# Two layers of attention and MLP on one core: the first row blocks of layer 1 pass over the keys in two spans instead of three

## The chip, the cores and the metric

One core of a Trainium2 chip runs the whole kernel. The metric is the device time of one execution in microseconds. Each time is a median of several runs; the profile is of one further execution, whose own time stands beside its span.

The engines are named as the profile names them: PE is TensorE, ACT is ScalarE, DVE is VectorE, POOL is GpSimd, SP is SyncE, whose queue (SPq) issues the DMAs here.

## The reference

The input x has 2048 rows of 448 columns. Two layers with the same weights are applied to it. Each adds an attention with 16 heads of 28 columns, and then an MLP with 1792 hidden columns.

```python
x = A_x
x = x + _A_ref(_layernorm(x, axis=-1), A_wqkv, A_wo)
x = x + _B_ref(_layernorm(x, axis=-1), B_w1, B_b1, B_w2, B_b2)
x = x + _A_ref(_layernorm(x, axis=-1), A_wqkv, A_wo)
x = x + _B_ref(_layernorm(x, axis=-1), B_w1, B_b1, B_w2, B_b2)
# _A_ref: qkv = x @ wqkv, p = softmax(q k^T * 28 ** -0.5), (p v) @ wo
# _B_ref: h = relu(x @ w1 + b1), (h * h) @ w2 + b2
```

Every one of the 2048 rows of a layer attends to all 2048 keys of that layer. A key of layer 1 exists only when layer 0 has finished that row, attention and MLP.

## The kernel before

**Tiling.** Rows are taken in row blocks of 256 (`blocks`, L242; the last two of layer 1 have 128), keys in 16 key blocks of 128. The 16 heads are four groups `g` of four heads `hh`, which lie on 32 partitions each. A *unit* is the scores of one head for a row block against two key blocks: 512 columns. Three units make one score tile `sc` of 1,536 columns in PSUM, of which there are two buffers. One exponential of ACT (L834) turns such a tile into `pt` in SBUF. There are 2,048 units in the two layers, and 683 tiles.

**Some units go to DVE.** `apart` (L703) can take one unit of a tile away from ACT: DVE then computes the exponential itself with a polynomial, in six instructions (L892, L904, three times L909, L915), and ACT gets a tile of 1,024 columns. `apart` allows it when DVE has been idle enough lately (`pl.load(SPAN, "DVE")`), with a lower bound when the MLP work is behind its line (`behind`, L688, with `LINES`).

**Passes.** `add_passes` (L652) lists the passes: a pass is one row block, one head group and one range of key blocks. A pass runs the units of its range, and then multiplies their exponentials with V into one PSUM tile `oT` (PV, L982). If the range is not the last one of the row block, `ev` (L996) moves `oT` to SBUF, into a part of `K_sb` of the other layer (`part`, L289): the first range copies (L1005), the later ones add (L1007). The last range adds the parts to `oT_sb`. Row blocks 0, 1 and 2 of layer 1 (`AHEAD`, L52) run over the keys in ranges given by `CUTS` (L93, L662): all three row blocks and four head groups over the first range, then all over the second, and so on. In this way layer 1 can begin while layer 0's MLP still makes the later keys. The other row blocks run over all 16 key blocks at once.

**After the last range** of two head groups, `norm_pair` (L1068) divides by the softmax's sum: a small DMA spreads the sums over partitions (`dn<-oT_sb`, L1080), DVE takes the reciprocal (L1085), a DMA writes it to DRAM (`scr<-dn`, L1091), another brings it back on all partitions (`rec<-scr`, L1099), and DVE multiplies (L1104). When the four groups are done, `chain` (L1116) does the rest of the layer for the row block: output projection, addition to x (L1113), layer norm (statistics L448, `rstd` on POOL L471, L520, transposes L493, copy L505), hidden layer (w1 on PE at L553, relu L1160, square L1167), w2, addition to x. In layer 0 it goes on to K, V and Q of layer 1 (L575, L603, L571).

**What sets the order.** `Planner` (L124) goes through all streams of work while the program is built. It keeps a clock for each engine, gives every operation a start from its inputs and its buffers, and emits them in that order; the instruction streams of all engines are fixed then, and each engine runs its own in order. The score stream has the first priority, ACT's exponentials the second, the PV stream (`p_stream`, L932) the third; MLP and projections fill in. A score tile needs its keys and queries (`needs`, L739) and a free `sc` buffer. Where PE has been idle lately, the score matmuls of a tile are issued again (`again`, L797), or matmuls with the identity are put in (`heat`, L1203, L1218): they change no result and keep PE busy.

Of the kernel before, what the change touches and what calls it, by code (L numbers as in the profile page):

```python
# [89 lines left out]
HSTOP = 0  # L90
CHUNK = 2
EV = 3.5
CUTS = (0, 8, 12, 16)  # L93


class Res:
# [121 lines left out]
def kernel(  # L218
# [433 lines left out]
    def add_passes(l, qbs, cuts, gs=range(G)):  # L652
        for lo, hi in zip(cuts, cuts[1:]):
            for qb in qbs:
                for g in gs:
                    passes.append((l, qb, g, range(lo, hi), lo == 0, hi == NTB))
# [3 lines left out]
    for qb in range(2, len(blocks[0])):  # L660
        add_passes(0, [qb], [0, 16])
    for cut in zip(CUTS, CUTS[1:]):  # L662
        for qb, gs in enumerate(AHEAD):
            add_passes(1, [qb], cut, gs)
        if cut[1] == CUTS[-2]:
            bridged = len(passes)
# [602 lines left out]
```

The softmax here doesn't subtract the row's maximum and nothing guards it: scores larger than these inputs give would overflow.

## Time and profile before

| | |
|---|---|
| median of 4 runs | 896.29 us (894.43 to 897.07) |
| profiled execution, its own time | 895.43 us |
| its span | 893.6 us |
| DVE busy | 794.0 us in 1,572 instructions |
| PE busy | 830.6 us in 12,829 matmuls |
| POOL busy | 39.0 us |
| all DMA | 18.43 MB, 21 GB/s on average |
| L834, full tiles | 555, of 1,536 columns |
| L834, short tiles | 128, of 1,024 columns |
| first exponential begins, last one ends | 9.4 and 877.6 us |

The exponentials are numbered 0 to 682 below in the order in which ACT runs them; the score tiles have the same numbers. Number 341 is the first with units of layer 1. In the profile, a row of the groups gives line, engine, operation, what is written and read with its shape, how often; then busy time, mean duration of one, and the idle time of that engine before it with what ended it. A duration of one exponential includes a part that overlaps the next one, so the distance of two starts is shorter than it.

### The profile page before, as it was taken

To read this page: it belongs to the slowest core of one execution; us is meant where nothing else is said; L and a number is where in the kernel's file an instruction comes from. 1 tells how busy PE (TensorE), PEld (TensorE's weight loads), DVE (VectorE), ACT (ScalarE), POOL (GpSimd) and SP (SyncE) were. 2 spreads that over 40 slices of the span, in tenths; PEclk is the share of its full clock that TensorE was granted. 3 is DMA by queue.
4 is the path that set the end of the run, shared out by engine and by line. 5 is a ranking of instruction groups with operands and counts; after the bars stand their busy time and mean duration, and the time that the engine had idled before them with its cause. 6 is when DMAs were issued, how large, how long until landed. Compare 5 with 4: busy or idle time off the path is not lost.

```text
span 893.6 us, 29098 instructions
## 1 busy us (share of the span) xinstructions
PE 830.6 (93%) x12829; PEld 458.3 (51%) x12829; DVE 794.0 (89%) x1572; ACT 878.8 (98%) x707; POOL 39.0 (4%) x98
## 2 busy tenths in 40 slices
PE   8999999998999999999989998888999999999998
PEld 4555654554545545454554554444544544545566
DVE  7988999999889999999889999889898999989654
ACT  8999999999999999999999999999999999999995
POOL 3100000000000000100000000001000000000000
PEclk9999999999999999999999999999999999999999
DMA  9100100000000000000000000011000000000100
GB/s 266 35 3 3 27 19 11 14 14 15 14 3 14 15 14 14 14 11 6 2 2 2 2 2 2 3 39 38 11 18 19 20 25 19 20 8 19 32 14 18
DMA packets 33915, 18.43 MB, mean 21 GB/s; under 512 B 18874, under 2 KB 33339, under 8 KB 33788
## 3 DMA queue, kind: packets, MB, share of 16 engines
q1 hardware_dynamic: 33788, 16.58, 6.6%
q8 instruction: 100, 1.64, 0.8%
q14 instruction: 27, 0.22, 0.1%
HBM read 14.26 MB, written 2.07 MB: 18 GB/s over the span
## 4 chain that ended last, share of the span: by engine, by line
ACT 68%; issue 12%; PE 11%; DVE 7%; DMA 2%; SPq 1%; POOL 0%; DVEq 0%
ACT pt L834 68%; PE mt L553 4%; PE sc L809 3%; PE oT L982 2%; DVE v_h L909 1%; DVE K_sb L909 1%; DVE r L1160 1%; DMA rec<-scr 1%; PE sc L553 1%; DVE st L448 1%; DVE oTn L1104 0%; SPq L303 0%; DMA dn<-oT_sb 0%; DMA x_sb<-in_A_x_dram 0%; DVE oT_sb L1007 0%
## 5 line engine op out<-in xcount | busy, mean ns | idle before, releaser
L834 ACT ACTIVATE pt<-sc 128x1536 bf16<-128x1536 f32 (+1 forms) x683 | 863.9, 1569 | 2.4 <-PE sc L809 2.1
L809 PE MATMUL sc<-Q_sb,K_sb 32*128 32x256 bf16 (+1 forms) x5848 | 324.9, 265 | 53.6 <-ACT pt L834 48.0
L809 PEld LDWEIGHTS <-K_sb 32*128 32x128 bf16 x5848 | 157.6, 92 | 229.7 <-issue 201.1
L982 PE MATMUL oT<-pt,V_sb 128*32 128x256 bf16 (+1 forms) x4094 | 151.9, 268 | 0.6 <-DVE xnT L505 0.3
L553 PE MATMUL mt<-xnT,w 128*128 128x256 bf16 (+1 forms) x928 | 120.6, 269 | 0.9 <-DVE r L1160 0.5
L982 PEld LDWEIGHTS <-V_sb 128*32 128x32 bf16 x4352 | 91.7, 96 | 47.3 <-issue 44.3
L909 DVE SCALAR_TENSOR_TENSOR K_sb<-K_sb 128x512 f32<-128x512 uint16 x165 | 112.9, 685 | 0.9 <-PE mt L553 0.2
L909 DVE SCALAR_TENSOR_TENSOR v_h<-v_h,v_i 128x512 f32<-128x512 f32 x144 | 98.2, 682 | 0.6
L553 PEld LDWEIGHTS <-w 128*128 128x128 bf16 x952 | 78.6, 98 | 35.5 <-issue 27.2
L1160 DVE TENSOR_SCALAR r<-mt 128x512 bf16<-128x512 f32 x106 | 72.2, 681 | 14.8 <-PE mt L553 14.5
L553 PE MATMUL mt<-w,V_sb 128*128 128x448 bf16 (+2 forms) x288 | 67.6, 345 | 0.0
L892 DVE TENSOR_SCALAR v_i<-sc 128x512 int32<-128x512 f32 x72 | 49.3, 685 | 9.7 <-PE sc L809 9.3
L1113 DVE TENSOR_TENSOR x_sb<-x_sb,mt 128x448 bf16<-128x448 bf16 (+2 forms) x63 | 37.8, 605 | 13.4 <-PE mt L553 13.4
L909 DVE SCALAR_TENSOR_TENSOR v_h<-v_i 128x512 f32<-128x512 uint16 x72 | 49.1, 682 | 0.5
L470 POOL TENSOR_TENSOR ve<-mv,eps_t 128x2 f32<-128x2 f32 (+1 forms) x34 | 8.8, 260 | 840.8 <-DVE mv L449 840.8
L1218 PE MATMUL mt<-xn,ident 128*128 128x448 bf16 x130 | 43.5, 357 | 0.5 <-DVE x_sb L1113 0.3
L892 DVE TENSOR_SCALAR K_sb<-sc 128x512 int32<-128x512 f32 x55 | 37.6, 684 | 4.5 <-PE sc L809 4.3
L448 DVE BATCH_NORM_STATS2 st<-x_sb 128x6 f32<-128x448 bf16 x64 | 39.4, 615 | 1.4 <-DMA x_sb<-in_A_x_dram 1.2
L553 PEld LDWEIGHTS <-V_sb 128*128 128x128 bf16 x302 | 24.8, 98 | 25.5 <-issue 11.2
L915 DVE SCALAR_TENSOR_TENSOR V_sb<-v_h,v_e 128x512 bf16<-128x512 f32 x46 | 31.4, 682 | 0.3
L1167 DVE TENSOR_TENSOR V_sb<-r 128x512 bf16<-128x512 bf16 (+1 forms) x69 | 28.7, 417 | 2.1 <-ACT r L1158 1.5
L904 DVE TENSOR_SCALAR v_e<-v_i 128x512 int16<-128x512 int16 x72 | 30.1, 418 | 0.0
(106 smaller groups left out, 733.4 us busy)
## 6 DMA issues: line engine op xcount, KB each, us to landing
rec<-scr SPq DMA_DIRECT2D x56, 128.0 KB
x_sb<-in_A_x_dram SPq DMA_DIRECT2D x8, 224.0 KB
out_dram<-x_sb SPq DMA_DIRECT2D x15, 112.0 KB
w<-in_B_w_dram SPq DMA_DIRECT2D x1, 1568.0 KB
w<-in_B_w_dram SPq DMA_DIRECT2D x1, 1344.0 KB
dn<-oT_sb SPq DMA_DIRECT2D x56, 4.0 KB
V_sb<-in_A_wqkv_dram SPq DMA_DIRECT2D x4, 168.0 KB
scr<-dn SPq DMA_DIRECT2D x28, 8.0 KB
```

Of the source, the lines that this page charges most:

```text
L448: nc.vector.bn_stats(out=st[:, :], in_=x_sb[:, t0 + j, :])
L553: nc.tensor.matmul(box["t"][:, c0:c0 + n], lhsT=lhsT() if callable(lhsT) else lhsT, rhs=rhs, start=a, stop=b)
L809: nc.tensor.matmul(dst[k][:, i * nt * P:(i + 1) * nt * P], lhsT=K_sb[l][rows, g, (kb + i) * P:(kb + i + 1) * P], rhs=Q_sb[rows, g, t0 * P: ...
L834: t = nc.scalar.activation(out=pt[:, 0:n], in_=gbuf[gi]["sc"][:, 0:n], func=AF.Exp, scale=float(np.log(2.0)) * 2.0 ** -FRAC)
L892: t = nc.vector.tensor_scalar(out=box["i"], in0=two(src), scalar1=EXP_BIAS, scalar2=EXP_LOW, op0=ALU.add, op1=ALU.max)
L904: nc.vector.tensor_scalar(out=box["e"], in0=box["n"], scalar1=128.0, scalar2=128.0 * EXP_FIELD, op0=ALU.mult, op1=ALU.add)
L909: nc.vector.scalar_tensor_tensor(out=box["h"], in0=box["f"] if begin else box["h"], scalar=b, in1=box["f"], op0=ALU.add, op1=ALU.mult)
L915: nc.vector.scalar_tensor_tensor(out=box["two"](pd), in0=box["h"], scalar=b0, in1=box["e"].bitcast(DT.bfloat16), op0=ALU.add, op1=ALU.mult)
L982: nc.tensor.matmul(box["t"][DHP * hh:DHP * hh + DHP, 0:n], lhsT=V_sb[l][:, kb + i, 4 * g + hh, :], rhs=p[:, c0:c0 + n], start=begin and kb ...
L1113: nc.vector.tensor_tensor(out=x_sb[:, tb, lo:hi], in0=x_sb[:, tb, lo:hi], in1=t[:, 0:hi - lo], op=ALU.add)
L1160: nc.vector.tensor_scalar(out=r[:, 0:w], in0=t[:, 0:w], scalar1=0.0, scalar2=None, op0=ALU.max)
L1218: nc.tensor.matmul(t[:, 0:D], lhsT=ident[:, :], rhs=xns[0][:, 0:D], start=True, stop=True)
```

## The change

```diff
--- before.py
+++ after.py
@@ -90,7 +90,7 @@
 HSTOP = 0
 CHUNK = 2
 EV = 3.5
-CUTS = (0, 8, 12, 16)
+CUTS = (0, 10, 16)
```

Row blocks 0, 1 and 2 of layer 1 now run over key blocks 0 to 9 first, and then over 10 to 15. Before, they ran over 0 to 7, then 8 to 11, then 12 to 15. Each of the 12 pairs of row block and head group thus has two passes instead of three: one copy and one addition instead of one copy and two additions. The planner then orders everything after the first tiles of layer 1 anew.

## Prediction

> **What bounds the kernel now.** I read the page's busy table first, then the chain, then the exponentials by shape.
>
> ```profile
> PE 830.6 (93%) x12829; PEld 458.3 (51%) x12829; DVE 794.0 (89%) x1572; ACT 878.8 (98%) x707; POOL 39.0 (4%) x98
> ACT 68%; issue 12%; PE 11%; DVE 7%; DMA 2%; SPq 1%; POOL 0%; DVEq 0%
> ...
> L834 ACT ACTIVATE pt<-sc 128x1536 bf16<-128x1536 f32 x555 | 776.0, 1649 | 1.8 <-PE sc L809 1.5 <-ACT pt L834 0.2
> L834 ACT ACTIVATE pt<-sc 128x1024 bf16<-128x1024 f32 x128 | 147.9, 1225 | 0.6 <-PE sc L809 0.6
> ```
>
> ScalarE (ACT) is the bound: busy for 878.8 of 893.6 us, nearly all of it in the 683 exponentials of L834. PE at 93% is no second bound, because some of its work is filler (score matmuls of L809 issued again, identity matmuls of L1218). So only three things can move the time: how many units of 512 columns ACT exponentiates, how long ACT stands still between exponentials, and the stretch after the last one. One unit handed to VectorE shortens an exponential from 1,649 to 1,225 ns, so it is worth 0.42 us; the starts in the timeline say the same (1.33 us after a full tile, 0.905 us after a shorter one).
>
> Then I looked for ACT's lost time in the half that the change touches. I number the exponentials 0 to 682 in their order. Layer 1 begins at 341, so all before that stands as it was: the two builds' orders first differ at score group 344 (448 us). The busy time by stretches (columns: length, PE, PEld, DVE, ACT, POOL, granted clock, DMA share, GB/s):
>
> ```profile
> 580.00:590.00 10.00, 8.33 (x136) 3.86 (x136) 9.94 (x21) 10.00 (x9) 0.00 (x0) 1.00 0.12 30
> 590.00:600.00 10.00, 8.23 (x144) 4.70 (x145) 7.46 (x17) 9.74 (x9) 0.00 (x0) 1.00 0.18 51
> 600.00:610.00 10.00, 8.72 (x136) 4.26 (x124) 9.96 (x21) 9.48 (x8) 0.00 (x0) 1.00 0.14 35
> ...
> 630.00:640.00 10.00, 9.36 (x152) 5.08 (x150) 10.00 (x21) 9.68 (x8) 0.00 (x0) 1.00 0.02 4
> ```
>
> ACT falls short only around 600 and 636 us. By starts, exponentials 460 to 479 take 592.78 to 619.38, 26.60 us, where 17 full and 3 short ones at 1.33 and 0.905 make 25.33: **1.27 us lost**. Exponentials 480 to 499, of the same mix, take 26.27: 0.94 lost. The timeline of VectorE, PE and ACT tells why for the first:
>
> ```profile
> 589.99 0.42 DVE L1007 TENSOR_TENSOR oT_sb<-oT,K_sb 128x256 f32<-128x256 f32 x1
> 590.17 1.13 SPq L1080 DMA_DIRECT2D dn<-oT_sb  x2
> 594.36 0.25 DVE L1085 RECIPROCAL dn<-dn 128x16 f32<-128x16 f32 x1 [1.82 <-DMA dn<-oT_sb]
> 598.14 0.68 DVE L915 SCALAR_TENSOR_TENSOR pd<-K_sb,v_e 128x512 bf16<-128x512 f32 x1
> 598.88 0.27 PE L982 MATMUL oT<-pd,V_sb 128*32 128x256 bf16 x1 [0.80 <-DVE pd L915]
> 599.93 1.02 ACT L834 ACTIVATE pt<-sc 128x1024 bf16<-128x1024 f32 x1 [0.26 <-PE sc L809]
> ```
>
> VectorE reaches the reciprocal of a normalization before its DMA has landed and stands 1.82 us; the exponential that it was computing itself (L915) is late behind it, the PV matmul on PE waits 0.80 us for that, the scores queued behind the PV matmul are late, and ACT idles. It happens where VectorE has no slack: its instructions in the order of exponentials 450 to 469, at their start-to-start times (0.60 us for L909 and its like, 0.33 for L1007), are 24.3 us against 24.2 us of ACT.
>
> **What the change removes.** Row blocks 0, 1 and 2 of layer 1 make 24 passes instead of 36, so 12 of the L1007 additions into K_sb go. This row is that operation:
>
> ```profile
> L1007 DVE TENSOR_TENSOR K_sb<-oT,K_sb 128x256 f32<-128x256 f32 x28 | 11.7, 416 | 3.2 <-PE oT L982 3.1
> ```
>
> 12 x 0.33 = 4.0 us of VectorE, none of it on ACT's path by itself. The matmuls of scores (repeats aside) and of PV, the DMAs and GpSimd's instructions are as many as before. The planner fills the room: in the changed build's order, ACT has 553 full and 130 short exponentials (before 555 and 128), so VectorE takes 129 units instead of 127. ACT gains 2 x 0.42 = **-0.85 us**. VectorE pays 2 x (5 x 0.60 + 0.33) = 6.7 us, plus 0.6 us for one relu of the end that moves from ACT to it: +3.3 us net on an engine at 89%, spread over 440 us.
>
> PE issues 92 fewer repeated score matmuls and 15 more identity ones: filler, in gaps. Here a rule speaks against the change. The Trainium skill (TensorE: Matmul & The Clock Gate, Part 1 and "HAM oscillation") says that a PE idle for a window of about 3.4 us falls to half clock. By the rule, a stretch such as exponentials 440 to 459, with 12.0 us of real PE work in 24.6 us, depends on its filler; at half clock its 0.88 us of score and PV matmuls for an exponential would become 1.8 us against 1.33, about 1.1 us lost for each such window. The row says a granted clock of 1.00 in every stretch, and in that stretch the repeated scores are more than before (252 score matmuls). I take 0.
>
> **What it moves: the end of the first passes.** Each pass of the last span is 12 units (4 exponentials) instead of 8 (2.7). Two passes make one normalization, so these come every 8 exponentials (10 us) instead of 5.3 (6.7 us), each with its DMAs dn, scr and rec and its two VectorE steps. In the new order VectorE's densest 20 exponentials of layer 1 are 380 to 399 (24.3 us in 25.1), then 460 to 479 (23.9 in 25.5) and 410 to 429 (22.8 in 24.2): no 20 are full. The first row block's MLP also starts some 10 exponentials earlier, where PE and VectorE had room. So I take the 1.27 us as gone: **-1.27 us**. This rests on the DMA's real delay: from the end of L1007 (590.41) to the reciprocal (594.36) the row shows 3.95 us. The skill's fixed cost of about 2.0 us (DMA: Bandwidth & Descriptors, "Anatomy of one DMA", given for another issuing path) would have had it land before VectorE arrived at 592.5; by it there was no such wait to remove, and the gain would be 0. I take the row. Ends: 0 and -2.2 (the 0.94 goes as well; I leave it, since the same w1 and relu work comes in any case).
>
> **What it moves: keys 14 and 15 of layer 1.** The second span now holds keys 10 to 15, so keys 14 and 15 are needed at exponential 424 instead of 439, 15 x 1.26 = 19 us earlier. The chain that makes them (w2 matmul, L1113, statistics, GpSimd, transposes, L505, wk matmul, L575) is moved forward, but only by 10: L575 stands at group 423 instead of 433. Its cover of 6 exponentials (7.6 us) shrinks to 1. Sum, from the end of exponential 421: release 0.2, PE late by 0.35 behind 24 PV matmuls, scores 423 0.33, four wk matmuls 0.52, semaphore 0.1, L575 0.68, semaphore 0.1, scores 424 0.33, to ACT 0.25: 2.86 against 2 x 1.33 = 2.66. **+0.2 us**. Queued on PE behind the waiting scores are wv matmuls and then PV; the values are needed only passes later. Ends: 0, and 0.2 plus whatever VectorE is late at that point. Keys 8 to 13 are early enough (8 and 9 written at 293, needed at 346; 12 and 13 at 392, needed at 422).
>
> **The end.** After the last exponential six w1 matmuls that stood before it now stand behind it (6 x 0.065 = 0.39), and the relu on VectorE stands ahead of the L1113 that feeds the last normalization. **+0.4 us**; ends 0 and 1.0.
>
> **Sum:** -0.85 - 1.27 + 0.2 + 0.4 = -1.5 us. The profiled execution took 895.43 us, which becomes 893.9; it lay 0.86 under the median of the runs, 896.29, from which the forecast is 894.8.
>
> **Rivals.** *More is freed:* the 0.94 goes too, no wait for keys, no later end: -0.85 - 2.2 = -3.1, 893.2. For it: the passes hold PE's result banks for 12 fewer evictions. Against: the relu work is the same. *A stall for a stall:* the new order has a full spot (470 to 479, 13.6 us of VectorE in 13.0) and loses there what it gains at 600: -0.85 + 0.2 + 0.4 = -0.25, 896.0. *Slower:* VectorE is late at exponentials 420 to 429 (12.4 us of work in 11.7), the keys' chain with its six VectorE steps queues behind it in order, and since the cover is gone each microsecond is paid on ACT at 424. With the two longest VectorE waits of this stage, 1.82 for dn and 1.3 for PV, and no gain at 600: -0.25 + 3.1 = +2.9, 899.2. It decides from about 2 us of lateness. Against it: in the trace L575 runs at 559.95 and 568.83, just where its place in the order (groups 433 and 441, 559.4 and 569.2) puts it, so this chain is not late now. That the change does not do what it says is excluded by the order.
>
> **How the numbers follow.** A measurement here tells 0.2% (1.8 us) from no change: below 894.5 is faster, above 898.1 slower. Forecast 0.50 (893.3 to 896.3, 0.22 of it below 894.5); more freed 0.20, all faster; stall for a stall 0.06, same; slower 0.24. Faster 0.42, same 0.34, slower 0.24. The range reaches 0.8 us under the second case and just short of the last one's 899.2; what lies outside is 1 in 10 on each side.
>
> **What would show it.** Right: 553 and 130 rows of L834; ACT at 10.00 around 600 us; no ACT idle over 0.3 us at exponential 424 (548 us); a stretch after the last exponential of some 16.4 us (877.6 to 893.6 before). Wrong: ACT idle of over 1 us before 424 with PE waiting for K_sb L575, or new waits of PE for L915 or L1160 after 590 us.

## The result, and the profile after

The change takes 894.23 us (median of 28 runs, 892.78 to 896.56) against 895.54 us before (46 runs, 894.28 to 900.35): a ratio of 0.9985, with an interval of 0.9979 to 0.9991. That is 1.3 us less, where the prediction's sum was -1.5. The profiled execution took 893.35 us, its span is 891.6 us.

The busy table and the chain of the changed kernel, then its exponentials by shape (count, busy time, mean duration in ns, idle time before them):

```profile
PE 829.6 (93%) x12752; PEld 455.4 (51%) x12752; DVE 796.6 (89%) x1573; ACT 876.9 (98%) x706; POOL 39.1 (4%) x98
ACT 74%; issue 11%; PE 10%; DVE 3%; SPq 0%; DMA 0%; POOL 0%; ACTq 0%
```

```profile
L834 ACT ACTIVATE pt<-sc 128x1536 bf16<-128x1536 f32 x553 | 775.8, 1673 | 1.2 <-PE sc L809 1.1
L834 ACT ACTIVATE pt<-sc 128x1024 bf16<-128x1024 f32 x130 | 152.6, 1257 | 0.0
```

ACT still sets the time. Two full tiles have become short ones, and the idle time before the exponentials has gone from 2.4 to 1.2 us (1.8 + 0.6 before, 1.2 + 0.0 after). On the chain, VectorE has fallen from 7% to 3% and ACT risen from 68% to 74%: the chain now runs through fewer of VectorE's results. The busy time by stretches (columns as before: length, PE, PEld, DVE, ACT, POOL, granted clock, DMA share, GB/s):

```profile
590.00:600.00 10.00, 9.36 (x171) 5.17 (x166) 9.16 (x19) 10.00 (x9) 0.00 (x0) 1.00 0.11 29
600.00:610.00 10.00, 8.89 (x115) 4.22 (x113) 9.28 (x20) 10.00 (x10) 0.00 (x0) 1.00 0.07 17
...
630.00:640.00 10.00, 9.28 (x131) 4.04 (x120) 9.85 (x20) 10.00 (x9) 0.88 (x2) 1.00 0.05 14
```

Both places where ACT fell short, around 600 and around 636 us, are full (10.00 of 10). VectorE is no longer at 9.96 and 10.00 there.

The timeline at keys 14 and 15, now first needed by score tile 424 (start, duration, engine, line; idle time before it and its releaser in brackets):

```profile
546.91 0.42 DVE L1005 COPY K_sb<-oT 128x256 f32<-128x256 f32 x1
547.26 0.69 DVE L575 CAST K_sb<-mt 128x512 bf16<-128x512 f32 x1
547.38 0.92 PE L553 MATMUL mt<-wv,xnT 128*128 128x448 bf16 x4 [0.16 <-DVE K_sb L1005]
548.23 0.12 PEld L809 LDWEIGHTS <-K_sb 32*128 32x128 bf16 x7 [0.37 <-DVE K_sb L575]
```

The scores of 424 wait on PE until L575 has written the keys at 547.95, and start at 548.23. ACT loses 0.51 us here.

How the lost time is counted from here on: the distance between the starts of two exponentials, less 1.331 us after a full tile or 0.904 us after a short one. In these terms the change stands to before as follows (before's three numbers are the profile of the prediction and two further executions of the same program, below):

| us | before | change | difference of the means |
|---|---|---|---|
| start of the first exponential | 9.44, 9.64, 9.74 | 9.90 | +0.30 |
| lost, exponentials 0 to 343 | 7.47, 7.30, 7.20 | 7.18 | -0.14 |
| full / short tiles | 555 / 128 | 553 / 130 | -0.85 |
| lost, 404 to 423 (ends in the start of 424) | 0.13, 0.13, 0.13 | 0.75 | +0.62 |
| lost, 464 to 483 (around 600 us) | 1.27, 0.38, 1.39 | 0.20 | -0.81 |
| lost, 484 to 503 (around 630 us) | 0.93, 1.01, 1.13 | 0.28 | -0.74 |
| lost, the rest from 344 on | 3.41, 3.42, 3.41 | 2.92 | -0.49 |
| last exponential | 1.42, 1.42, 1.42 | 1.54 | +0.12 |
| after the last exponential | 16.03, 16.04, 16.05 | 16.14 | +0.10 |
| span | 893.6, 892.9, 894.0 | 891.6 | -1.9 |

### The profile page after: what moved, and what is told of

Same layout as the page of the kernel before. It is cut to its first block, busy times and chain, and to the rows that moved or that the text cites. A ratio compares the mean times of both kernels' runs of the same rounds, so it can differ in the third digit from the quotient of the medians.

```text
span 891.6 us, 28916 instructions
## 1 busy us (share of the span) xinstructions
PE 829.6 (93%) x12752; PEld 455.4 (51%) x12752; DVE 796.6 (89%) x1573; ACT 876.9 (98%) x706; POOL 39.1 (4%) x98
## 4 chain that ended last, share of the span: by engine, by line
ACT 74%; issue 11%; PE 10%; DVE 3%; SPq 0%; DMA 0%; POOL 0%; ACTq 0%
ACT pt L834 74%; PE mt L553 4%; PE sc L809 3%; PE oT L982 2%; PE sc L553 1%; DVE K_sb L909 0%; DVE r L1160 0%; SPq L303 0%; DMA x_sb<-in_A_x_dram 0%; DVE st L448 0%; PE mt L1218 0%; DVE v_h L909 0%; PE tp L493 0%; DVE v_e L904 0%; DVE K_sb L892 0%
## 5 line engine op out<-in xcount | busy, mean ns | idle before, releaser
L809 PE MATMUL sc<-Q_sb,K_sb 32*128 32x256 bf16 (+1 forms) x5756 | 320.6, 265 | 53.7 <-ACT pt L834 47.5
L809 PEld LDWEIGHTS <-K_sb 32*128 32x128 bf16 x5756 | 153.6, 92 | 231.7 <-issue 203.4
L909 DVE SCALAR_TENSOR_TENSOR K_sb<-K_sb 128x512 f32<-128x512 uint16 x168 | 114.8, 683 | 0.7 <-PE mt L553 0.2
L1160 DVE TENSOR_SCALAR r<-mt 128x512 bf16<-128x512 f32 (+1 forms) x107 | 73.0, 682 | 14.8 <-PE mt L553 14.5
L892 DVE TENSOR_SCALAR v_i<-sc 128x512 int32<-128x512 f32 x73 | 50.0, 685 | 11.8 <-PE sc L809 11.0
L1218 PE MATMUL mt<-xn,ident 128*128 128x448 bf16 x145 | 48.5, 356 | 1.1 <-DVE oT_sb L1005 0.3
L1113 DVE TENSOR_TENSOR x_sb<-x_sb,mt 128x448 bf16<-128x448 bf16 (+2 forms) x63 | 37.9, 603 | 11.8 <-PE mt L553 11.8
L892 DVE TENSOR_SCALAR K_sb<-sc 128x512 int32<-128x512 f32 x56 | 38.3, 685 | 5.9 <-PE sc L809 5.5
L915 DVE SCALAR_TENSOR_TENSOR V_sb<-v_h,v_e 128x512 bf16<-128x512 f32 x43 | 29.4, 683 | 0.3
```

Source lines behind the costliest of these rows:

```text
L809: nc.tensor.matmul(dst[k][:, i * nt * P:(i + 1) * nt * P], lhsT=K_sb[l][rows, g, (kb + i) * P:(kb + i + 1) * P], rhs=Q_sb[rows, g, t0 * P: ...
L892: t = nc.vector.tensor_scalar(out=box["i"], in0=two(src), scalar1=EXP_BIAS, scalar2=EXP_LOW, op0=ALU.add, op1=ALU.max)
L909: nc.vector.scalar_tensor_tensor(out=box["h"], in0=box["f"] if begin else box["h"], scalar=b, in1=box["f"], op0=ALU.add, op1=ALU.mult)
L915: nc.vector.scalar_tensor_tensor(out=box["two"](pd), in0=box["h"], scalar=b0, in1=box["e"].bitcast(DT.bfloat16), op0=ALU.add, op1=ALU.mult)
L1113: nc.vector.tensor_tensor(out=x_sb[:, tb, lo:hi], in0=x_sb[:, tb, lo:hi], in1=t[:, 0:hi - lo], op=ALU.add)
L1160: nc.vector.tensor_scalar(out=r[:, 0:w], in0=t[:, 0:w], scalar1=0.0, scalar2=None, op0=ALU.max)
```

## Experiments

What had to be told apart: is the time around 600 us gained because normalizations come further apart (the prediction's reason), because VectorE has 12 additions fewer, or because the planner's new order happens to lie better? And why did the earlier need for keys 14 and 15 cost so little? Each experiment changes a constant or a line or two of the kernel; the ratios are against the kernel before on the same chip.

### The changed kernel again

> The changed kernel once more, for its own spread and its granted clock run by run. If the profiled gain of 2.1 us is the whole effect, runs with a mean granted clock of 1.000 lie near 893.3 in this kernel and near 895.4 in the one before, and the medians differ by about 2. If the change also costs clock (less filler, half-clock windows), this kernel shows more runs below 1.000 than the one before, and the medians differ by 1.3 or less.

893.89 us, ratio 0.9987 (0.9979 to 0.9995): the gain holds. Its runs at a granted clock of 1.000 have a median of 893.20 us, those of the kernel before beside them 894.61: 1.4 us, and not the 2.1 us between the two profiles. Its profiled execution ran at a mean granted clock of 0.996. Two stretches of it show where:

```profile
200.00:220.00 20.00, 18.06 (x275) 9.21 (x276) 18.59 (x38) 18.95 (x16) 1.06 (x4) 0.91 0.06 16
860.00:880.00 20.00, 18.65 (x387) 11.33 (x386) 7.64 (x18) 16.66 (x14) 0.75 (x2) 0.91 0.04 14
```

The clock is 0.91 in each, from one piece of 3.4 us at half clock (at 213.5 and 875.7 us in the clock's record); ACT is busy for 18.95 of 20 us in the first. The second begins under the last exponential, and the stretch behind that one is 17.64 us instead of 16.14. This comes back under the clock, below.

### The kernel before, twice more

> The kernel before, profiled once more. If the loss of 1.27 us in exponentials 464 to 483 belongs to its order, it is there again (over 1 us). If it was one execution's late DMA, ACT loses less than 0.5 us there this time and the span at a granted clock of 1.000 is 892.8, 0.8 under the profile that the prediction was made from; then of the 2.0 us between the two profiles only about 1.3 belong to the change.

> The same once more: a loss of over 1 us in exponentials 464 to 483 if it belongs to the order, less than 0.5 us if it comes and goes with the landing of the dn DMA. The loss of 0.9 us in 484 to 503 is expected in both looks.

894.63 and 895.76 us, both at a granted clock of 1.00. VectorE's wait at the reciprocal and the stretch around 600 us, in the first:

```profile
DVE dn L1085 <- DMA dn<-oT_sb: 0.9, 1, 0.9
```

```profile
600.00:610.00 10.00, 8.61 (x137) 4.63 (x136) 9.96 (x21) 9.90 (x9) 0.00 (x0) 1.00 0.11 30
```

and in the second:

```profile
DVE dn L1085 <- DMA dn<-oT_sb: 1.9, 1, 1.9
```

```profile
600.00:610.00 10.00, 8.72 (x136) 4.39 (x135) 9.96 (x21) 9.40 (x8) 0.00 (x0) 1.00 0.15 39
```

The same instructions in the same order: where the wait is 1 us shorter, ACT idles 0.10 us in this stretch instead of 0.60, and exponentials 464 to 483 lose 0.38 us instead of 1.39. SyncE's queue shows where the difference comes from. It issues the broadcast of the normalization before (`rec<-scr`) at these times, in the prediction's profile and in the two repeats:

```profile
589.05 1.07 SPq L1099 DMA_DIRECT2D rec<-scr  x2
588.17 1.07 SPq L1099 DMA_DIRECT2D rec<-scr  x2
588.88 1.07 SPq L1099 DMA_DIRECT2D rec<-scr  x2
```

It had stood there until that normalization's write `scr<-dn` (L1091, issued at 585.7 in all three) had landed. The `dn` DMA comes next in the queue, at 590.17, 589.29 and 590.00. From there to the reciprocal it is 4.2, 4.2 and 4.5 us. In the first repeat, then, the whole difference lies in the earlier write, which held the queue 0.9 us less.

So the stall on which most of the prediction's sum rested is not a constant of the kernel. The profile before happened to show it near its larger size. The loss around 630 us is about 1.0 us in all three.

### Before, with the reciprocal placed later

The planner is told that the small DMA of the first three row blocks lands 2 us later, so that it puts L1085 further down VectorE's stream. Nothing else is edited.

```diff
-        d1 = Op("DMA", 0.9, spread, deps=pair["ev"], lat=1.0)
+        d1 = Op("DMA", 0.9, spread, deps=pair["ev"], lat=3.0 if l == 1 and qb < 3 else 1.0)
```

> The kernel before with its three spans, but the planner counts 2 us more for the dn DMA of row blocks 0 to 2 of layer 1, so that L1085 stands later in VectorE's order; the 555 and 128 exponentials stay. Theory A (the wait of VectorE at L1085 starts the stall): no wait of VectorE for dn over 0.3 us, and ACT loses less than 0.5 us in exponentials 464 to 483 instead of 1.27; ratio 0.998 to 0.9995. Theory B (the stall is only too much VectorE work in the last span): 1 us or more is still lost there, ratio 0.9995 to 1.001.

894.85 us, ratio 0.9995 (0.9988 to 1.0003). VectorE waits for `dn` nowhere, and exponentials 464 to 483 lose 0.21 us; 484 to 503 still lose 1.03. The stretches around 600 and 636 us:

```profile
600.00:610.00 10.00, 8.63 (x130) 4.48 (x124) 9.95 (x20) 10.00 (x9) 0.00 (x0) 1.00 0.18 55
630.00:640.00 10.00, 8.81 (x159) 5.00 (x148) 9.97 (x21) 9.57 (x8) 0.00 (x0) 1.00 0.02 4
```

The wait at L1085 does start the stall at 600 us: with the wait gone ACT is full there, although VectorE still is busy 9.95 of 10. But the median hardly moves: its interval goes from 1.1 us less to 0.3 us more. This neither shows nor excludes the 0.8 us of the stall, and gives no sign that the stall alone makes the change's gain.

### Three spans as 6, 4 and 6 key blocks

```diff
-CUTS = (0, 8, 12, 16)
+CUTS = (0, 6, 10, 16)
```

> Three spans of 6, 4 and 6 key blocks: all 48 additions of L1007 as before, but the last span as long as in the change. Theory A (the spacing of the normalizations in the last span removes the stalls after 590 us): ACT loses less than 0.5 us in exponentials 464 to 483 and the time is that of the change (ratio 0.998 to 0.999). Theory B (the 12 additions fewer remove them): ACT loses 1 us or more there as before, ratio 0.999 to 1.001. Both: keys 14 and 15 are written one score tile ahead of their use as in the change, so about 0.5 us is lost at 424.

907.81 us, ratio 1.0138 (1.0121 to 1.0154). As many passes as before, and the last span of the change. No theory of the stall at 600 us had the time right, since something else happened, at the first use of keys 14 and 15:

```profile
543.32 5.72 ACT L834 ACTIVATE pt<-sc 128x1536 bf16<-128x1536 f32 x4
554.00 0.69 DVE L575 CAST K_sb<-mt 128x512 bf16<-128x512 f32 x1 [1.17 <-PE mt L553]
554.75 1.04 PE L809 MATMUL sc<-Q_sb,K_sb 32*128 32x256 bf16 x12 [0.79 <-DVE K_sb L575]
555.46 1.94 ACT L834 ACTIVATE pt<-sc 128x1024 bf16<-128x1024 f32 x2 [6.42 <-PE sc L809]
```

ACT ends its exponentials at 549.0 and stands for 6.42 us, because L575 comes at 554.00 instead of 547.26. Tile 424 is the first to need these keys, as in the change, and L575 stands at tile 423 of the order, as in the change. What differs is VectorE's work before it: from 448 us to this L575 it runs 24 evictions (L1005, L1007), in the change 12, and otherwise the same instructions but for one more L915 and one L892 less. The stretch after the last exponential is 20.46 us. Exponentials 464 to 483 lose only 0.29.

### Two spans as 12 and 4

```diff
-CUTS = (0, 8, 12, 16)
+CUTS = (0, 12, 16)
```

> Two spans of 12 and 4 key blocks: 36 additions as in the change, the last span as short as before. Theory A: the normalizations come every 5.3 exponentials, a reciprocal or its DMA holds up VectorE, and ACT loses about 1 us in the last span's end (exponentials 455 to 490); ratio near 0.9995. Theory B: less than 0.5 us lost there, ratio 0.998 to 0.999. Both: keys 14 and 15 are written at tile 425 and needed at 438, so nothing is lost for them.

900.02 us, ratio 1.0058 (1.0041 to 1.0075). The passes of the last span are as short as before, so normalizations come every 5.3 exponentials as before, and yet 464 to 483 lose 0.21 and 484 to 503 lose 0.41; VectorE waits for `dn` for 0.3 us in all. **The spacing by itself does not make the stall.** The loss of 12 and 4 is at the end, in ACT's timeline:

```profile
866.62 8.19 ACT L834 ACTIVATE pt<-sc 128x1536 bf16<-128x1536 f32 x6
883.05 0.60 ACT L1158 ACTIVATE r<-sc 128x512 bf16<-128x512 f32 x1 [8.24 <-PE sc L553]
```

The last exponential ends at 874.81, as early as any, but the stretch behind it is 23.42 us instead of 16.03. ACT stands 8.24 us before the relu of the last row blocks. The planner has left MLP work for the end: the three additions to x (L1113) that in the kernel before lie 14.3, 7.8 and 6.3 us before the end of the last exponential lie 9.2 and 1.5 us before and 1.5 us after it. A piece of 3.4 us at half clock, at 881.0 us, falls into this wait too.

### 12 and 4 with a steeper line for the MLP

`LINES` says how much MLP work should be done by when; from a tile that is behind, DVE takes units more rarely.

```diff
-CUTS = (0, 8, 12, 16)
-LINES = ((280, 1312, 7.8), (1440, 2040, 7.0))
+CUTS = (0, 12, 16)
+LINES = ((280, 1312, 7.8), (1440, 2040, 7.4))
```

> Spans of 12 and 4 key blocks with the MLP's line of layer 1 raised from 7.0 to 7.4 row blocks, so that VectorE takes fewer units when the MLP is behind (125 instead of 129, 1.7 us more for ACT). Theory A (12 and 4 was slow because the MLP of the last row blocks was behind at the end): the stretch after the last exponential falls from 23.4 to 16 to 17 us and the time to 894 to 895.5. Theory B (the end is long for another reason of 12 and 4): the stretch stays over 20 us and the time over 899.

894.94 us, ratio 0.9994 (0.9986 to 1.0003). The first relu behind the exponentials, in ACT's timeline:

```profile
878.09 0.60 ACT L1158 ACTIVATE r<-mt 128x512 bf16<-128x512 f32 x1 [1.23 <-PE mt L553]
```

It waits 1.23 us instead of 8.24, and the end is back at 16.04 us. So the +0.6% of 12 and 4 was in the main MLP work left for the end. The exponentials lose 4.09 us from 344 on, as in the change (4.15), but 557 of them are full and 126 short, against 553 and 130: 4 x 0.427 = 1.7 us more on ACT. That is the difference to the change (its span is 892.9, 1.3 longer).

### The change with the first span's copies made twice

This doubles L1005 for the first span of row blocks 0 to 2, and the planner is told its length.

```diff
-                    nc.vector.tensor_copy(out=dst, in_=src)
+                    [nc.vector.tensor_copy(out=dst, in_=src) for _ in range(2 if l == 1 and qb < 3 else 1)]
...
-            oe = Op("DVE", 0.15 + n / 930, ev, deps=[o], rel=box["o"])
+            oe = Op("DVE", (0.15 + n / 930) * (2 if first and l == 1 and qb < 3 else 1), ev, deps=[o], rel=box["o"])
```

> The change, with each of the 12 copies out of the first span made twice (the planner counts both): VectorE gets back the 4 us that the removed additions gave it, with no pass or PSUM bank more. Theory A (the VectorE time of the additions is what lets keys 14 and 15 come in time for the second span): the last L575 comes 3 to 7 us later than 547 and 553 us, ACT loses 3 to 7 us at exponential 424 instead of 0.5. Theory B (the passes and their banks, not VectorE's time, decide): the loss at 424 stays under 1 us.

907.55 us, ratio 1.0134 (1.0120 to 1.0149). The timeline at tile 424:

```profile
542.61 6.58 ACT L834 ACTIVATE pt<-sc 128x1536 bf16<-128x1536 f32 x5
552.03 1.86 PE L553 MATMUL mt<-xnT,wk 128*128 128x256 bf16 x8 [1.53 <-DVE xnT L505]
553.93 0.69 DVE L575 CAST K_sb<-mt 128x512 bf16<-128x512 f32 x1 [1.95 <-PE mt L553]
555.98 1.94 ACT L834 ACTIVATE pt<-sc 128x1024 bf16<-128x1024 f32 x2 [6.79 <-PE sc L809]
```

Twelve copies of 0.33 us are 4.0 us of VectorE. From 448 us to L575 VectorE runs 190 instructions instead of 177: the twelve copies and one more L915, the others are the same. L575 is 6.7 us late (553.93 instead of 547.26), and ACT stands 6.79 us. About 4.6 us of this are the 13 instructions, by their start distances, and 1.3 us more waits of VectorE among them, the largest the 1.95 us for PE above; the rest was not told apart. The other half of the 13 us that the kernel loses lies at the end: behind the last exponential come 22.80 us instead of 16.14, as in 12 and 4.

So the additions that the change takes away do not speed anything up by themselves, but in these orders the earlier need for keys 14 and 15 is met only where this room is there.

### Two spans of 8 key blocks

```diff
-CUTS = (0, 8, 12, 16)
+CUTS = (0, 8, 16)
```

> Two spans of 8 and 8 key blocks: as many additions as in the change, but keys 14 and 15 needed at tile 409 instead of 424, about 19 us earlier. Theory A: VectorE is overfull before (24 to 30 us of work in 25 us at tiles 389 to 410), the keys cannot be there, ACT loses 8 to 20 us at 405 to 410, ratio 1.01 to 1.025. Theory B (two spans are better than three, wherever the cut): ratio under 1.000.

911.25 us, ratio 1.0179 (1.0165 to 1.0193), though it too has only 24 passes. ACT's timeline where the second span begins, at exponential 409:

```profile
524.50 5.17 ACT L834 ACTIVATE pt<-sc 128x1024 bf16<-128x1024 f32 x4
542.70 3.44 ACT L834 ACTIVATE pt<-sc 128x1024 bf16<-128x1024 f32 x3 [13.03 <-PE sc L809]
```

Keys are needed 15 exponentials earlier than in the change, some 19 us, and L575 comes only 6.7 us earlier, at 540.60: 13.03 us of standing. The stretch behind the last exponential is 20.46 us. This is the prediction's rival of late keys, at full size.

### Three spans as 10, 2 and 4

```diff
-CUTS = (0, 8, 12, 16)
+CUTS = (0, 10, 12, 16)
```

> Three spans of 10, 2 and 4 key blocks: all 48 additions, the first span as long as in the change, keys 14 and 15 needed at 438 instead of 424 (written at 424). 554 and 129 exponentials, 0.43 us more for ACT than in the change. Theory A (the wait for keys and the end decide, the additions by themselves cost little): nothing over 0.2 us lost at any span's beginning, the stretch after the last exponential 16 us, ratio 0.998 to 0.9995. Theory B (the 12 additions are the gain by themselves): ratio 1.000 or more.

893.35 us (12 runs), ratio 0.9981 (0.9973 to 0.9990): as fast as the change, with a span of 891.7. It has all of the additions that the change removes (L1007 adds into K_sb 28 times, as before; 16 times in the change), and keys 14 and 15 are first needed at tile 438. It loses 4.03 us from 344 on, with no single wait over 0.3 us, has 554 full and 129 short tiles, and 16.04 us at the end. **Fewer additions are not needed for the gain.** What it shares with the change is a first span of 10 and a new order.

### The change with the first line of the MLP steeper

```diff
-LINES = ((280, 1312, 7.8), (1440, 2040, 7.0))
+LINES = ((280, 1280, 7.8), (1440, 2040, 7.0))
```

> The change, with the line of layer 0's MLP ended at unit 1280 instead of 1312: the MLP counts as behind earlier and VectorE takes fewer units there, so that keys 14 and 15 are written at tile 419 instead of 423 while they are needed at 424 as before; the rest is planned anew with 552 and 131 exponentials. Theory A (the 0.5 us at 424 is the wait for these keys): under 0.15 us lost at 424 and, with one unit fewer on ACT (0.42), a time about 0.9 us under the change if the end stays at 16 us: ratio 0.9975. Theory B (the 0.5 us has another cause at the change of spans, such as the banks): it stays.

897.70 us, ratio 1.0031 (1.0020 to 1.0041). The wait at 424 is gone (404 to 423 lose 0.30 instead of 0.75), so it was the wait for these keys, but 200 to 299, where layer 0's MLP is now pressed, lose 4.38 instead of 1.19, and a new wait of 1.7 us stands at 516. The 0.5 us at 424 cannot be had in this way.

### The change without filler

```diff
-MORE = 3
-HEAT = 0.74
+MORE = 0
+HEAT = 0.0
```

> The change without filler: score matmuls are not issued again and no identity matmuls are put in (the results are the same; 554 and 129 exponentials). If PE needs the filler for its clock, the mean granted clock falls well under 0.99, PE's real work takes up to twice as long in those stretches, and the time rises by several us (about 1.3 us for each stretch of 3.4 us at half clock). If real work alone keeps the clock, it stays at 0.996 to 1.000 and the time within 0.3% of the change.

No score matmul is repeated and no identity matmul put in. 921.23 us, ratio 1.0293 (1.0277 to 1.0308). The busy table, and one of the stretches:

```profile
PE 795.1 (87%) x11203; PEld 411.5 (45%) x11203; DVE 794.2 (86%) x1567; ACT 882.0 (96%) x706; POOL 39.4 (4%) x98
```

```profile
560.00:580.00 20.00, 13.93 (x215) 5.82 (x206) 17.53 (x33) 19.55 (x17) 0.00 (x0) 0.68 0.04 9
```

The same stretch of the change shows 17.30 us of PE and a clock of 1.00. Here PE is busy for 13.93 of 20 us, and the granted clock is 0.68. Over the execution the clock is 0.927: 21 stretches, together 133 us, at half clock. The kernel is 27 us slower than the change, which is 0.2 us for each of these if all of it is put down to the clock; 4.6 of the 27 lie behind the last exponential. PE never stands idle for more than 1.4 us here after its start, but in the 3.4 us before each of the 21 stretches it is busy for only 27 to 64% of the time.

## Why the prediction was right, and where its steps were not

The sum was right in sign and nearly in size. The expected time lay 1.5 us under the runs then known, the measured difference is 1.3, and the time itself is 894.2 where 894.8 was predicted. The table above shows that it was made up of other sizes: that the sum fits so closely is luck in part.

**Two units to VectorE, -0.85.** Right: 553 and 130 rows, and the start distances of 1.33 and 0.905 us held.

**The stall at 600 us, -1.27.** The place and the beginning were right: the experiment with the later reciprocal shows that the wait at L1085 starts it. The term was mis-sized, since one execution was taken for the kernel: the three profiles of before lost 1.27, 0.38 and 1.39 us, the change 0.20, so that -0.8 was there to gain. The reading of the wait was wrong in one step, too. The addition at 589.99 from which the prediction counted 3.95 us belongs to the next pair: in the first repeat both `dn` DMAs were issued from 589.29 on, before that addition began (590.02). The pair's own second addition ended at 587.66. Then the DMA stood in SyncE's queue behind `rec<-scr` until 590.17, and 4.2 us passed to the reciprocal, 6.7 in all. So the 3.95 us are not the DMA's delay, and what was weighed against them settles nothing.

The reason for the stall's going, normalizations every 8 exponentials instead of every 5.3, is not enough. The queue does stand on the normalization before, which was only 4.4 us ahead (L1091 at 581.3 and 585.7), and in the change none is under 7 us behind another. But 12 and 4 keeps the old spacing and has no stall, and in 10-2-4, where two lie 3.3 us apart and the queue stands 3.6 us between L1091 and L1099, VectorE does not wait for `dn`. What can be said is that the stall belongs to one order, in which a reciprocal stands too near its DMA where VectorE is full. Of the other choices of spans, 12-4, 6-4-6 and 10-2-4 do not have it (0.21 to 0.29 us), the last two with as many additions as before; 8-8, whose late keys shift everything behind them, loses 0.88 us there, with no wait at L1085 near. This is a consequence of replanning, and no property of two spans.

**The 0.94 us "I leave, since the same w1 and relu work comes in any case".** This step failed. It went almost whole: 484 to 503 lose 0.28 us. It went in all four other choices of spans too (0.08 to 0.41), and it stayed (1.03) where only the reciprocal was moved. The same work does come, but elsewhere: between 610 and 640 us VectorE has six relus of L1160 in the kernel before and four in the change, and it was full there (10.00 of 10). But 12-4 and 10-2-4 have seven there, and ACT is full (30.00 of 30), so the number of relus is not the reason. Why ACT stood there stays open. The rival that more is freed was right in this point.

**Keys 14 and 15, +0.2.** Measured +0.5 to +0.6, above the 0.3 that the prediction gave as the sign of being right, and far from the 1 us that would have shown it wrong. What fails is how it was worked out. The prediction read the cover from the order: L575 one tile ahead of its use. But L575 stands at tile 423 also in 6-4-6 and with the doubled copies, where ACT loses 6.8 and 7.1 us. The planner emits a tile's scores after its keys, however long ACT must stand for them, so the order shows this place in any case. What decides is what VectorE has to run before it: twelve evictions more, 4.0 us of work, brought L575 6.7 us late in both. "Slower" named this mechanism and gave it 2 us of lateness as the point from which it decides. How few evictions more would have been too many was not tried, but the room is small: in the change's order exponentials 410 to 429 hold 24.1 us of VectorE's work, by the start distances, in 24.1 us of ACT, where the prediction counted 22.8 in 24.2. On this side the saved additions do count.

**The end, +0.4.** Measured +0.1. The six matmuls and the relu do come later, but what can lengthen the stretch by much more is MLP work left for the end, and none is left here; 12 and 4 shows what it costs when some is (+7.4).

**The clock, 0.** In the profiled execution, right: the clock is 1.00 everywhere. The rule that was weighed there, of the Trainium skill (TensorE: Matmul & The Clock Gate, Part 1), names an idle window of about 3.4 us as what halves the clock. The run without filler shows that the filler is needed, but not for this reason: PE was never idle for more than 1.4 us, and the clock fell after windows in which PE was busy for 64% or less. In the repeated change it fell after two windows with PE busy for 2.23 and 2.17 of 3.41 us. So the prediction was right to fear for a stretch with 12.0 us of PE work in 24.6, though the rule as it reads does not say it. The clock also takes something back from the gain. Of 50 runs of the changed kernel 22 had a clock of 1.000 (median 893.25 us), 20 had 0.998 (894.55) and 8 had 0.996 (895.96), so each piece of 3.4 us at half clock costs about 1.3 us. Of 70 runs of the kernel before, 45 had 1.000 (894.84) and 21 had 0.998 (895.98). At equal clock the change gains 1.6 us over all these runs (1.4 on the one chip of the repeat); its runs have 0.72 such pieces on average against 0.44, so some 0.3 to 0.4 us is given back, which leaves about the 1.3 of the medians. Whether the changed order is to blame stays open: of the two pieces in the profile of the repeated kernel, one lies at 213 us, where both kernels have the same instructions, and the other at the last exponential.

**Still open:** the 0.74 us around 630 us and the 0.49 us gained in small amounts over the rest of layer 1, which have no single place. And whether a first span of 10 is better than 8 for a reason, or because two orders made with it (the change, and 10-2-4) lie well, was not settled. The two differ by less than their intervals.

## What to carry to other kernels

Look at several executions before you price a stall that begins at a DMA: here one and the same wait was 0.9, 1.8 or 1.9 us, and the stall behind it 0.4 to 1.4. Then look at what stands before that DMA in its queue: here an earlier DMA's landing held it back. Where instructions are ordered by a planner, the place of an instruction says only that it stands ahead of its use; whether it is in time is read from what the in-order engine must run before it, and a small surplus there (4.0 us of VectorE) can come back larger (6.7 us) at the deadline. Such an edit moves everything behind it, so try other values of the same constant, read the stretch after the last exponential by itself, and do not put down to the edit what any new order brings.

## What the hardware showed that was not expected

- The clock falls in pieces: 3.4 us in a single one, 6.8 and 10.2 us (two and three times that) in or behind the long waits for keys of the doubled copies, of 8-8 and of 6-4-6. The medians of the change's runs with none, one and two such pieces lie about 1.3 and 1.4 us apart, as much as the whole change.
- The clock fell also in a kernel where PE is busy for 93% of the span: 28 of 50 runs of the change had at least one such piece. No idle gap of 3.4 us is needed for it: the longest of PE in the repeated change is 0.9 us, and before its two pieces PE was busy for 65 and 64% of 3.4 us.
- The wait for the same DMA, at the same place in the order, differed by 1 us between executions of one program. In the repeat with the short wait the DMA itself was not faster (4.2 us from its issue to the reciprocal in both); it was issued 0.9 us earlier, since the write that the queue stood on landed earlier.
